# Products of two blocks of F in the second half of the opening, and the last six of the 32 steps of x's first transform stage left to the h/dh pass

## The chip, the cores and the metric

One core of a Trainium2 chip runs the kernel. The metric is device time in microseconds (us). Engines: PE is TensorE, DVE is VectorE, ACT is ScalarE, POOL is GpSimd. DMAs are issued from SP's and POOL's queues. "Granted clock" is the share of TensorE's full clock; it is taken from the trace.

## The reference, cut to what matters

```python
x = A_x
g = sigmoid((x * gate_w).sum(-1, keepdims=True))
a = irfft2(rfft2(x) * (w_r + 1j * w_i))          # spectral branch, S x D = 2048 x 1024
h = relu(x @ w1 + b1) ** 2                        # dense branch, F = 3584
b = h @ w2 + b2
out = g * a + (1 - g) * b
# returned: out, and the gradients of x, w_r, w_i, w1, b1, w2, b2, gate_w for a given grad_out
```

Both branches work on x (A_x); the input B_x takes no part. The kernel needs h and its gradient dh for all of F. It works them out in 14 blocks of 256 columns of F, each in 4 steps s of 512 rows, with 2 halves c.

## The kernel before: the parts that matter

Four stretches follow each other. In the **opening** (to about 85 us) x and grad_out come in, are scaled, transposed on PE into xT and dbT, and x's first transform stage (`first_stage_of_x`, 16 tiles) runs beside block 0 of the dense branch. A row step of that stage is some additions on DVE (the folds) and 8 products on PE; a column step is 8 products on PE, copies on ACT, two additions on DVE (the **u additions**) and a store of u to DRAM (the **z store**, `z_scr`). Two buffers hold u, so a u addition can have to wait for an earlier z store. In the **h/dh pass** the other blocks run beside the first stage of the gradient. Then come the pw products (weight gradients) beside the spectral middle, and at last the outputs.

```python
def hidden(fc, ss, w1g, h2T):              # "ph": 8 products of 512 columns, then ACT
    ph = mps.tile([P, SW], FP32, name="ph", tag="ph", bufs=2)
    ...
    nc.scalar.activation(rT[:], ph[:], ACT.Relu, bias=...)
    nc.scalar.activation(h2T, rT[:], ACT.Square)

def grads(fc, sb, ss, rT, dhT):            # "pd": 8 products, then DVE; shares ph's two PSUM buffers
    pd = mps.tile([P, SW], FP32, name="pd", tag="ph", bufs=2)
    ...
    return STT(out=dhT, in0=pd[:], scalar=2.0, in1=rT[:], ...)

# opening, once for each 4 tiles i0
gate(i0); next(stage); next(units); next(stage)
for k in (i0 // 2, i0 // 2 + 1):
    turned(dbT, k, ...); next(stage)       # transposes of dbn on PE, copies dbT<-pt on DVE
... x_pair(k), next(stage) twice           # transposes of x, copies on ACT
next(units); next(stage); next(stage)
# after it
for _ in stage: pass
first = first_stage_of_grad()
mixed = spread(units, first, 0.55)         # 0.55 side steps for each unit of the dense branch
while n < 78: ...
```

At fixed steps of a block, DVE also transposes h2T, dhT and w1 for later stages, and the w2 of the next group (a group is two blocks of F): `load_w2` loads it (`w2r`), `turn_group` turns it on DVE, `move` writes it over the w2T of this group.

Of the kernel before, what the change touches and what calls it, by code (L numbers as in the profile page):

```python
# [10 lines left out]
P = 128  # L11
BF16 = mybir.dt.bfloat16
# [113 lines left out]
def kernel(  # L126
# [22 lines left out]
    nc = tc.nc  # L149
# [7 lines left out]
    S2, DC, FC = g.S2, g.DC, g.FC  # L157
# [3 lines left out]
    FGW, FG, FGC = g.FGW, g.FG, g.FGC  # L161
# [55 lines left out]
    def after(ins, earlier, wait=mybir.DependencyClass.Sync):  # L217

        if earlier is not None:
            info = mybir.DependencyInfo(wait, mybir.DependencyReason.DATA)  # L220
            tc.add_manual_dep(ins.ins, earlier.ins.name, info, reason="paced")
# [420 lines left out]
    def mlp_in():  # L642
# [8 lines left out]
        def hidden(fc, ss, w1g, h2T):  # L651
            ph = mps.tile([P, SW], FP32, name="ph", tag="ph", bufs=2)
            for dc in range(DC):
                mm(ph[:], lhsT=w1g[:, dc, fc % 2 * P : (fc % 2 + 1) * P], rhs=xT[:, dc, ss], start=(dc == 0), stop=(dc == DC - 1))  # L654
            rT = wb.tile([P, SW], BF16, name="rT", tag="rT", bufs=3)
            nc.scalar.activation(rT[:], ph[:], ACT.Relu, bias=b1col[:, fc : fc + 1])  # L656
            nc.scalar.activation(h2T, rT[:], ACT.Square)  # L657
            return rT

        def grads(fc, sb, ss, rT, dhT):  # L660
            w_ = w2T[fc % FGC].bitcast(BF16)
            pd = mps.tile([P, SW], FP32, name="pd", tag="ph", bufs=2)
            for ec in range(DC):
                mm(  # L664
                    pd[:], lhsT=w_[:, ec // 2, ec % 2 :: 2], rhs=dbT[:, ec, ss],
                    start=(ec == 0), stop=(ec == DC - 1),
                )
            return STT(  # L668
                out=dhT, in0=pd[:], scalar=2.0, in1=rT[:], op0=ALU.mult, op1=ALU.mult,
                accum_out=gb1part[:, fc, sb : sb + 1],  # L670
            )
# [6 lines left out]
        def turn_w2(fc):  # L678
            w2r = wb.tile([P, D], BF16, name="w2n", tag="w2n", bufs=2)
            ld(out=w2r[:], in_=B_w2[fc * P : (fc + 1) * P, :])  # L680

            def turn():
                ptw = tps.tile([P, DC, P], BF16, name="ptw", tag="tr", bufs=2)
                for b in range(DC):
                    nc.tensor.transpose(ptw[:, b, :], w2r[:, of_tile(b)], identb[:])
                nc.vector.tensor_copy(
                    out=w2_tile(fc).bitcast(BF16).rearrange("p u (m c) -> p u c m", c=2),
                    in_=ptw[:].rearrange("p (u c) m -> p u c m", c=2),
                )

            return turn
# [19 lines left out]
                for b in range(4):  # L711
                    ld(out=t_[32 * b : 32 * (b + 1)], in_=v_[32 * a : 32 * (a + 1), :, b, :])

        for fp in range(FC // 2):
            w1g = wb.tile([P, DC, PW], BF16, name="w1g", tag="w1g", bufs=2)
            ld(out=w1g[:], in_=w1v[:, :, fp * PW : (fp + 1) * PW])
            fg, pr = divmod(fp, NPR)
            turns = []
            if fp == 0:
                turns = [turn_w2(0), turn_w2(1)]  # L720
            if fp == 0:
                yield
            step = 0
            for sp in range(2):
                cols2 = slice(2 * sp * SW, 2 * (sp + 1) * SW)
                h2T, dhT = (wb.tile([P, 2, 2 * SW], BF16, name=n_, tag=n_, bufs=2) for n_ in ("h2T", "dhT"))
                for sh in range(2):
                    sb = 2 * sp + sh
                    ss = slice(sb * SW, (sb + 1) * SW)
                    hs = slice(sh * SW, (sh + 1) * SW)  # L730
                    if fp == 0:
                        rT = [hidden(c, ss, w1g, h2T[:, c, hs]) for c in range(2)]
                        yield
                    for t_ in turns:
                        t_()
                    turns = []
                    if fp == 0 and sb == 1:
                        turns = [turn_w2(2), turn_w2(3)]
                    for c in range(2):
                        if fp > 0:  # L740
                            rT = {c: hidden(2 * fp + c, ss, w1g, h2T[:, c, hs])}
                        last = grads(2 * fp + c, sb, ss, rT[c], dhT[:, c, hs])
                        later["last"] = last
                        if 8 * pr + step == 3:
                            later["blocks"] = last
                        if step == 4:
                            st1 = wb.tile([P, 2, 4, DC, 32], BF16, name="stg1", tag="stg1", bufs=1)
                            turned_ = nc.vector.transpose(
                                out=st1[:].rearrange("p v b c i -> p c (v b) i"),
                                in_=w1g[:].rearrange("p c (b i) -> p c b i", i=32),  # L750
                            )
                            after(turned_, last, mybir.DependencyClass.NoSync)
                            st(
                                out=w1T_scr[2 * fp : 2 * fp + 2].rearrange("v p b r -> p v (b r)"),
                                in_=st1[:].rearrange("p v b c i -> p v (b c i)"),
                            )
                        if pr == 0 and step == 1 and fg > 0:
                            move((2, 3))
                        if fg + 1 < FG:
                            at = 8 * pr + step  # L760
                            if at == (7 if fg == 0 else 5):
                                for q in range(4):
                                    load_w2(fg + 1, q, last)
                            if at == 11:
                                for q in range(4):
                                    turn_group(q, last)
                                move((0, 1))
                        step += 1
                        if fp > 0 or c == 1:
                            yield  # L770
                stg = wb.tile([P, 16, 2, 32], I32, name="stg", tag="stg", bufs=3)
                for c in range(2):
                    nc.vector.transpose(  # L773
                        out=stg[:, :, c, :], in_=h2T[:, c, :].bitcast(I32).rearrange("p (b i) -> p b i", i=32)
                    )
                st(out=h2_scr[fg][:, 16 * sp : 16 * (sp + 1), 2 * pr : 2 * pr + 2, :], in_=stg[:])
                st(out=h2T_scr[2 * fp : 2 * fp + 2, :, cols2].rearrange("c p s -> p c s"), in_=h2T[:])
                stg = wb.tile([P, 4, 8, 2, 32], BF16, name="stgd", tag="stg", bufs=3)
                for c in range(2):
                    nc.vector.transpose(  # L780
                        out=stg[:, :, :, c, :].rearrange("p b k i -> p k b i"),
                        in_=dhT[:, c, :].rearrange("p (k b i) -> p k b i", b=4, i=32),
                    )
                st(
                    out=dh_scr[fg][:, :, pr, 8 * sp : 8 * (sp + 1), :].rearrange("p b k r -> p b (k r)"),
                    in_=stg[:].rearrange("p b k c i -> p b (k c i)"),
                )
                st(out=dhT_scr[2 * fp : 2 * fp + 2, :, cols2].rearrange("c p s -> p c s"), in_=dhT[:])
        mpss.close()
        wbs.close()  # L790
        xT_s.close()
# [226 lines left out]
    for i0 in range(0, NT, 4):  # L1018
        for i in range(i0, i0 + 4):
            ld(out=dbn[:, i, :], in_=go_perm[i])  # L1020
        if i0 + 4 < NT:
            for i in range(i0 + 4, i0 + 8):
                xs[i] = source(i, x_perm)
        gate(i0)
        next(stage, None)
        next(units)
        next(stage, None)
        for k in (i0 // 2, i0 // 2 + 1):
            turned(dbT, k, lambda i: dbn[:, i, :], of_tile, nc.vector.tensor_copy)
            next(stage, None)  # L1030
        if i0 + 4 < NT:
            for k in (i0 // 2 + 2, i0 // 2 + 3):
                x_pair(k)
                next(stage, None)
        next(units)
        next(stage, None)
        next(stage, None)
    for _ in stage:
        pass
    V(out=gpg[:], in0=gcol[:], in1=omg[:], op=ALU.mult)  # L1040
    first = first_stage_of_grad()
    n = 0
    mixed = spread(units, first, 0.55)
    while n < 78:
        next(mixed)
        n += 1
    for _ in first:
# [53 lines left out]
```

## Time and profile before

| what | before |
|---|---|
| time, median of the first 3 runs | 1335.81 us (1335.26 to 1336.68) |
| span of the profiled run | 1334.6 us |
| PE busy | 1298.0 us (97%) |
| DVE busy in the opening, 29 to 81 us | 50.86 of 52 us |
| first pw product starts at | 466.45 us |

The page's busy shares name the bound of the whole; the busy time of each engine in a stretch names the bound of that stretch, and here it is another one. The prediction shows these lines. One tool is used: the **loss**, which is the start of an instruction in the trace less all PE work that stands before it in the built order, at the streaming durations that the prediction lists. A loss that grows between two points is PE time that stood, or ran slowly, between them. It needs starts alone; PE busy times are less sure, as some PE records can be missing from a trace (the page of before has 6974 products for 7082 weight loads).

### The profile page before, as it was taken

The numbers are of one execution on the slowest core, as the hardware profiler recorded it, in microseconds if no ns is written. First come the engines' busy times: TensorE is split into PE (matmuls) and PEld (weight loads), VectorE is DVE, ScalarE is ACT, GpSimd is POOL, SyncE is SP. The second block draws the span as 40 slices with busy tenths as digits, with TensorE's granted clock in tenths as the row PEclk, the third lists the DMA queues.
The fourth block names the chain that finished last, engine by engine and source line by source line (L and its number), as shares of the span: only waits on it lengthen the run. The fifth ranks groups of instructions, "written<-read, shape, count | busy, mean of one in ns | idle before, by whom it ended". The sixth has DMA issues, their size and how long they took to land.

```text
span 1334.6 us, 18965 instructions
## 1 busy us (share of the span) xinstructions
PE 1298.0 (97%) x6974; PEld 630.2 (47%) x7082; DVE 836.0 (63%) x1669; ACT 424.5 (32%) x722; POOL 295.7 (22%) x484
## 2 busy tenths in 40 slices
PE   7889999999999999999999999999999899999998
PEld 4644444444444444444444445555444444444443
DVE  6986777676666596785667863434756776842232
ACT  6863555555433323232332323443111111000000
POOL 0222232232222253533442212121000000000000
PEclk9999999999999999999999999999999999999999
DMA  7547787788768988889886557778888854663530
GB/s 274 188 161 242 242 254 255 236 259 247 242 207 241 278 252 186 215 201 218 215 174 180 145 156 231 234 251 250 207 223 218 246 163 136 206 180 97 147 103 24
DMA packets 217094, 273.06 MB, mean 205 GB/s; under 512 B 16988, under 2 KB 152170, under 8 KB 217002
## 3 DMA queue, kind: packets, MB, share of 16 engines
q1 hardware_dynamic: 181306, 153.58, 43.4%
q0 software_dynamic: 35696, 118.27, 27.3%
q8 instruction: 55, 0.90, 0.3%
q14 instruction: 37, 0.30, 0.1%
HBM read 146.99 MB, written 118.51 MB: 199 GB/s over the span
## 4 chain that ended last, share of the span: by engine, by line
PE 83%; DVE 9%; DMA 3%; issue 2%; ACT 1%; POOL 1%; SPq 0%; DVEq 0%; ACTq 0%; POOLq 0%
PE accg L983 14%; PE acc L941 14%; PE pw L875 14%; PE ph L654 13%; PE pd L664 13%; PE pw L858 7%; DMA out_dram<-wo 2%; DVE dbacc L835 1%; PE pui L283 1%; DVE dbT L579 1%; PE pki L504 1%; PE pk L250 1%; DVE x L332 1%; PE pu L283 1%; DVE t L451 1%
## 5 line engine op out<-in xcount | busy, mean ns | idle before, releaser
L654 PE MATMUL ph<-xT,w1g 128*128 128x512 bf16 x869 | 215.6, 382 | 2.1 <-DMA w1g<-in_B_w_dram 0.7
L664 PE MATMUL pd<-dbT,w2T 128*128 128x512 bf16 x876 | 211.5, 381 | 3.9 <-DVE dhT L668 1.8
L875 PE MATMUL pw<-grd,res 128*128 128x512 bf16 x896 | 202.4, 379 | 0.0
L858 PE MATMUL pw<-dbn,grp 128*128 128x512 bf16 x875 | 199.9, 379 | 1.2 <-issue 0.2
L941 PE MATMUL acc<-w,hblk 128*128 128x512 bf16 x874 | 196.4, 379 | 3.0 <-DVE bGo L943 1.8
L983 PE MATMUL accg<-w1Tr,hblk 128*128 128x512 bf16 x878 | 192.9, 379 | 0.9
L664 PEld LDWEIGHTS <-w2T 128*128 128x128 bf16 x896 | 87.6, 98 | 107.8 <-issue 5.6
L983 PEld LDWEIGHTS <-hblk 128*128 128x128 bf16 x896 | 87.5, 98 | 105.8 <-issue 0.9
L858 PEld LDWEIGHTS <-grp 128*128 128x128 bf16 x896 | 86.8, 98 | 103.1 <-issue 0.9
L941 PEld LDWEIGHTS <-hblk 128*128 128x128 bf16 x896 | 86.6, 98 | 100.5 <-issue 1.9
L875 PEld LDWEIGHTS <-res 128*128 128x128 bf16 x896 | 86.0, 98 | 98.7 <-issue 0.7
L654 PEld LDWEIGHTS <-w1g 128*128 128x128 bf16 x896 | 86.1, 98 | 97.9 <-issue 2.1
L656 ACT ACTIVATE rT<-ph,b1col 128x512 bf16<-128x512 f32 x112 | 77.0, 687 | 142.6 <-PE ph L654 135.6
L668 DVE SCALAR_TENSOR_TENSOR dhT<-pd,rT 128x512 bf16<-128x512 f32 x112 | 75.1, 671 | 55.4 <-PE pd L664 46.0
L988 DVE TENSOR_TENSOR gxo<-accg,g 128x512 bf16<-128x512 f32 x32 | 22.1, 691 | 106.3 <-PE accg L983 100.7
L773 DVE STREAM_TRANSPOSE stg<-h2T 128x512 int32<-128x512 int32 x56 | 39.8, 711 | 64.4 <-ACT h2T L657 64.4
L862 ACT CAST wo<-pw 128x512 bf16<-128x512 f32 x56 | 32.7, 585 | 143.4 <-PE pw L858 127.5
L870 POOL DMA_DIRECT2D out_dram<-wo x112 | 56.0, 506 | 93.2 <-ACT wo L862 76.1
L880 ACT CAST wo<-pw 128x512 bf16<-128x512 f32 x56 | 32.8, 585 | 132.0 <-PE pw L875 103.0
L657 ACT ACTIVATE h2T<-rT 128x512 bf16<-128x512 bf16 x112 | 70.5, 630 | 3.1
L780 DVE STREAM_TRANSPOSE stgd<-dhT 128x1024 bf16<-128x1024 bf16 x56 | 69.3, 1240 | 1.2
L332 DVE TENSOR_TENSOR x<-px,common 128x1024 f16<-128x1024 f32 x32 | 38.8, 1220 | 45.3 <-ACT common L329 45.3
(182 smaller groups left out, 1488.8 us busy)
## 6 DMA issues: line engine op xcount, KB each, us to landing
h2T_scr<-h2T POOLq DMA_DIRECT2D x28, 512.0 KB, 4.6
h_scr<-stg POOLq DMA_DIRECT2D x28, 512.0 KB, 6.9
dhT_scr<-dhT POOLq DMA_DIRECT2D x28, 512.0 KB, 7.4
dh_scr<-stgd POOLq DMA_DIRECT2D x28, 512.0 KB, 7.1
grp<-h_scr SPq DMA_DIRECT2D x112, 128.0 KB
grd<-dh_scr SPq DMA_DIRECT2D x112, 128.0 KB
hblk<-h2T_scr SPq DMA_DIRECT2D x8, 1792.0 KB
hblk<-dhT_scr SPq DMA_DIRECT2D x8, 1792.0 KB
```

What stands on the lines that cost most here:

```text
L332: V(out=x[:, j, :, 0:H].rearrange("p c (i g) -> p c i g", g=4), in0=px[:].rearrange("p c (g i) -> p c i g", g=4), in1=common[:].rearrange( ...
L654: mm(ph[:], lhsT=w1g[:, dc, fc % 2 * P : (fc % 2 + 1) * P], rhs=xT[:, dc, ss], start=(dc == 0), stop=(dc == DC - 1))
L656: nc.scalar.activation(rT[:], ph[:], ACT.Relu, bias=b1col[:, fc : fc + 1])
L657: nc.scalar.activation(h2T, rT[:], ACT.Square)
L664: mm(pd[:], lhsT=w_[:, ec // 2, ec % 2 :: 2], rhs=dbT[:, ec, ss], start=(ec == 0), stop=(ec == DC - 1),)
L668: return STT(out=dhT, in0=pd[:], scalar=2.0, in1=rT[:], op0=ALU.mult, op1=ALU.mult, accum_out=gb1part[:, fc, sb : sb + 1],)
L780: nc.vector.transpose(out=stg[:, :, :, c, :].rearrange("p b k i -> p k b i"), in_=dhT[:, c, :].rearrange("p (k b i) -> p k b i", b=4, i=32),)
L858: mm(pw[:], lhsT=cur[:, t // 2, 2 * fb_ * P + t % 2 : 2 * (fb_ + 1) * P : 2], rhs=dbn[:, t, hf * H : (hf + 1) * H], start=(t == 0), stop=( ...
L870: st(out=dst[q], in_=wo[32 * q : 32 * (q + 1), :])
L875: mm(pw[:], lhsT=xr[t][:, d_ * P : (d_ + 1) * P], rhs=cur[:, t], start=(t == 0), stop=(t == NT - 1),)
L941: mm(acc[:], lhsT=cur[:, fc, t2::2], rhs=w2[:, fc, cs], start=(fc == 0), stop=(fc == FC - 1))
L983: mm(acc[:], lhsT=cur[:, fc, t2::2], rhs=w1T[:, fc, 2 * hf : 2 * hf + 2, :], start=(fc == 0), stop=(fc == FC - 1),)
```

## The change

PE waits for DVE in the opening and is full in the pass. So work that PE can do without much DVE is pulled forward from the pass, and work that costs DVE is pushed back. Core of the diff (cut; the bodies of `forth` and `back_` are the old loop's, taken apart):

```diff
+        for s in range(4):
+            both(forth, 0, s)                      # ph of block 0
+            yield
             ...
+            if s == 1:
+                load_w1(1)
+                turns = [turn_w2(2), turn_w2(3)]
+            if s >= 2:
+                both(forth, 1, s - 2)              # ph of block 1, first half
+            both(back_, 0, s)                      # pd of block 0
+            if s >= 2:
+                both(back_, 1, s - 2)              # pd of block 1, first half
+            yield
+        for fp in range(1, FC // 2):
+            ...
+            for s in range(2 if fp == 1 else 0, 4):
...
-                            if at == (7 if fg == 0 else 5):
+                if at == (4 if fg == 0 else 5):    # loads of the next group's w2
...
         next(units)
         next(stage, None)
-        next(stage, None)
-    for _ in stage:
-        pass
     V(out=gpg[:], in0=gcol[:], in1=omg[:], op=ALU.mult)
-    first = first_stage_of_grad()
+    def firsts():
+        yield from stage                           # what is left of x's stage: 4 column, 2 row steps
+        yield from first_stage_of_grad()
+    first = firsts()
-    mixed = spread(units, first, 0.55)
-    while n < 78:
+    mixed = spread(units, first, 0.62)
+    while n < 75:
```

More of the change, by code (lines that the diff above doesn't have):

```diff
@@ L712, in move @@
                     ld(out=t_[32 * b : 32 * (b + 1)], in_=v_[32 * a : 32 * (a + 1), :, b, :])
-        for fp in range(FC // 2):
-            w1g = wb.tile([P, DC, PW], BF16, name="w1g", tag="w1g", bufs=2)
-            ld(out=w1g[:], in_=w1v[:, :, fp * PW : (fp + 1) * PW])
-            fg, pr = divmod(fp, NPR)
-            turns = []
-            if fp == 0:
-                turns = [turn_w2(0), turn_w2(1)]
-            if fp == 0:
-                yield
-            step = 0
-            for sp in range(2):
-                cols2 = slice(2 * sp * SW, 2 * (sp + 1) * SW)
-                h2T, dhT = (wb.tile([P, 2, 2 * SW], BF16, name=n_, tag=n_, bufs=2) for n_ in ("h2T", "dhT"))
-                for sh in range(2):
-                    sb = 2 * sp + sh
-                    ss = slice(sb * SW, (sb + 1) * SW)
-                    hs = slice(sh * SW, (sh + 1) * SW)
-                    if fp == 0:
-                        rT = [hidden(c, ss, w1g, h2T[:, c, hs]) for c in range(2)]
-                        yield
-                    for t_ in turns:
-                        t_()
-                    turns = []
-                    if fp == 0 and sb == 1:
-                        turns = [turn_w2(2), turn_w2(3)]
-                    for c in range(2):
-                        if fp > 0:
-                            rT = {c: hidden(2 * fp + c, ss, w1g, h2T[:, c, hs])}
-                        last = grads(2 * fp + c, sb, ss, rT[c], dhT[:, c, hs])
-                        later["last"] = last
-                        if 8 * pr + step == 3:
-                            later["blocks"] = last
-                        if step == 4:
-                            st1 = wb.tile([P, 2, 4, DC, 32], BF16, name="stg1", tag="stg1", bufs=1)
-                            turned_ = nc.vector.transpose(
-                                out=st1[:].rearrange("p v b c i -> p c (v b) i"),
-                                in_=w1g[:].rearrange("p c (b i) -> p c b i", i=32),
-                            )
-                            after(turned_, last, mybir.DependencyClass.NoSync)
-                            st(
-                                out=w1T_scr[2 * fp : 2 * fp + 2].rearrange("v p b r -> p v (b r)"),
-                                in_=st1[:].rearrange("p v b c i -> p v (b c i)"),
-                            )
-                        if pr == 0 and step == 1 and fg > 0:
-                            move((2, 3))
-                        if fg + 1 < FG:
-                            at = 8 * pr + step
-                            if at == (7 if fg == 0 else 5):
-                                for q in range(4):
-                                    load_w2(fg + 1, q, last)
-                            if at == 11:
-                                for q in range(4):
-                                    turn_group(q, last)
-                                move((0, 1))
-                        step += 1
-                        if fp > 0 or c == 1:
-                            yield
-                stg = wb.tile([P, 16, 2, 32], I32, name="stg", tag="stg", bufs=3)
-                for c in range(2):
-                    nc.vector.transpose(
-                        out=stg[:, :, c, :], in_=h2T[:, c, :].bitcast(I32).rearrange("p (b i) -> p b i", i=32)
-                    )
-                st(out=h2_scr[fg][:, 16 * sp : 16 * (sp + 1), 2 * pr : 2 * pr + 2, :], in_=stg[:])
-                st(out=h2T_scr[2 * fp : 2 * fp + 2, :, cols2].rearrange("c p s -> p c s"), in_=h2T[:])
-                stg = wb.tile([P, 4, 8, 2, 32], BF16, name="stgd", tag="stg", bufs=3)
-                for c in range(2):
-                    nc.vector.transpose(
-                        out=stg[:, :, :, c, :].rearrange("p b k i -> p k b i"),
-                        in_=dhT[:, c, :].rearrange("p (k b i) -> p k b i", b=4, i=32),
-                    )
-                st(
-                    out=dh_scr[fg][:, :, pr, 8 * sp : 8 * (sp + 1), :].rearrange("p b k r -> p b (k r)"),
-                    in_=stg[:].rearrange("p b k c i -> p b (k c i)"),
-                )
-                st(out=dhT_scr[2 * fp : 2 * fp + 2, :, cols2].rearrange("c p s -> p c s"), in_=dhT[:])
@@ new lines, in mlp_in, with load_w1, forth @@
+        w1, h2, dh, rTs = {}, {}, {}, {}
+        wide = lambda n_: wb.tile([P, 2, 2 * SW], BF16, name=n_, tag=n_, bufs=2)
+        rows_ = lambda s: slice(s * SW, (s + 1) * SW)
+        def load_w1(fp):
+            w1[fp] = wb.tile([P, DC, PW], BF16, name="w1g", tag="w1g", bufs=2)
+            ld(out=w1[fp][:], in_=w1v[:, :, fp * PW : (fp + 1) * PW])
+        def forth(fp, s, c):
+            if c == 0 and s % 2 == 0:
+                h2[fp, s // 2], dh[fp, s // 2] = wide("h2T"), wide("dhT")
+            rTs[fp, s, c] = hidden(2 * fp + c, rows_(s), w1[fp], h2[fp, s // 2][:, c, rows_(s % 2)])
@@ new lines, in back_ @@
+        def back_(fp, s, c):
+            fg, pr = divmod(fp, NPR)
+            step = 2 * s + c
+            last = grads(2 * fp + c, s, rows_(s), rTs.pop((fp, s, c)), dh[fp, s // 2][:, c, rows_(s % 2)])
+            later["last"] = last
+            if 8 * pr + step == 3:
+                later["blocks"] = last
+            if step == 4:
+                st1 = wb.tile([P, 2, 4, DC, 32], BF16, name="stg1", tag="stg1", bufs=1)
+                turned_ = nc.vector.transpose(
+                    out=st1[:].rearrange("p v b c i -> p c (v b) i"),
+                    in_=w1[fp][:].rearrange("p c (b i) -> p c b i", i=32),
+                )
+                after(turned_, last, mybir.DependencyClass.NoSync)
+                st(
+                    out=w1T_scr[2 * fp : 2 * fp + 2].rearrange("v p b r -> p v (b r)"),
+                    in_=st1[:].rearrange("p v b c i -> p v (b c i)"),
+                )
+            if pr == 0 and step == 1 and fg > 0:
+                move((2, 3))
+            if fg + 1 < FG:
+                at = 8 * pr + step
+                if at == (4 if fg == 0 else 5):
+                    for q in range(4):
+                        load_w2(fg + 1, q, last)
+                if at == 11:
+                    for q in range(4):
+                        turn_group(q, last)
+                    move((0, 1))
+            if c == 1 and s % 2 == 1:
+                finish(fp, s // 2)
@@ new lines, in finish @@
+        def finish(fp, sp):
+            fg, pr = divmod(fp, NPR)
+            cols2 = slice(2 * sp * SW, 2 * (sp + 1) * SW)
+            h2T, dhT = h2.pop((fp, sp)), dh.pop((fp, sp))
+            stg = wb.tile([P, 16, 2, 32], I32, name="stg", tag="stg", bufs=3)
+            for c in range(2):
+                nc.vector.transpose(
+                    out=stg[:, :, c, :], in_=h2T[:, c, :].bitcast(I32).rearrange("p (b i) -> p b i", i=32)
+                )
+            st(out=h2_scr[fg][:, 16 * sp : 16 * (sp + 1), 2 * pr : 2 * pr + 2, :], in_=stg[:])
+            st(out=h2T_scr[2 * fp : 2 * fp + 2, :, cols2].rearrange("c p s -> p c s"), in_=h2T[:])
+            stg = wb.tile([P, 4, 8, 2, 32], BF16, name="stgd", tag="stg", bufs=3)
+            for c in range(2):
+                nc.vector.transpose(
+                    out=stg[:, :, :, c, :].rearrange("p b k i -> p k b i"),
+                    in_=dhT[:, c, :].rearrange("p (k b i) -> p k b i", b=4, i=32),
+                )
+            st(
+                out=dh_scr[fg][:, :, pr, 8 * sp : 8 * (sp + 1), :].rearrange("p b k r -> p b (k r)"),
+                in_=stg[:].rearrange("p b k c i -> p b (k c i)"),
+            )
+            st(out=dhT_scr[2 * fp : 2 * fp + 2, :, cols2].rearrange("c p s -> p c s"), in_=dhT[:])
@@ new lines, in mlp_in @@
+        both = lambda what, fp, s: [what(fp, s, c) for c in range(2)]
+        load_w1(0)
+        turns = [turn_w2(0), turn_w2(1)]
+        yield
+        for s in range(4):
+            both(forth, 0, s)
+            yield
+            for t_ in turns:
+                t_()
+            turns = []
+            if s == 1:
[6 more added lines that the diff above has]
+                both(back_, 1, s - 2)
+            yield
@@ L789, in mlp_in @@
+        for fp in range(1, FC // 2):
+            if fp > 1:
+                load_w1(fp)
+            for s in range(2 if fp == 1 else 0, 4):
+                for c in range(2):
+                    forth(fp, s, c)
+                    back_(fp, s, c)
+                    yield
         mpss.close()
```

## The prediction

> **What bounds the kernel now.** I read the page's busy shares first, then the stretches of time around the opening, then PE's and DVE's waits there, then PE's instructions in order of time.
>
> ```profile
> PE 1298.0 (97%) x6974; PEld 630.2 (47%) x7082; DVE 836.0 (63%) x1669; ACT 424.5 (32%) x722; POOL 295.7 (22%) x484
> ```
>
> PE (TensorE) is the bound over the whole, so only time in which PE stands or runs slowly can be won: 1334.6 - 1298.0 = 36.6 us in all. The stretches say where that lies (columns: stretch, length, busy of PE, PEld, DVE, ACT, POOL, granted clock, DMA share, GB/s):
>
> ```profile
> 29.00:81.00 52.00, 45.36 (x534) 31.90 (x540) 50.86 (x121) 39.49 (x86) 10.30 (x16) 1.00 0.57 191
> 81.00:99.50 18.50, 16.59 (x101) 8.44 (x101) 12.73 (x35) 10.96 (x23) 4.38 (x7) 0.91 0.47 151
> 99.50:130.00 30.50, 30.28 (x138) 13.78 (x141) 18.50 (x31) 11.15 (x17) 7.81 (x10) 1.00 0.82 250
> ```
>
> From 29 to 81 us, the opening, DVE is busy 50.86 of 52 us and PE stands 6.6 us: DVE is the bound there. From 99.5 us on, in the h/dh pass, PE is busy 30.28 of 30.5 and DVE only 18.5: PE is the bound and DVE has room. The waits before 100 us (us in total, times, longest) name it:
>
> ```profile
> PE pt L578 <- DVE dbT L579: 7.6, 9, 1.8
> PE pd L664 <- DVE dhT L668: 1.5, 1, 1.5
> ...
> DVE u L270 <- DMA z_scr<-u: 4.4, 1, 4.4
> ```
>
> PE's transposes of dbn/x wait for DVE to empty the two PSUM buffers (dbT copies, 1.13 us each from start to start). At the end of the opening PE's rows are
>
> ```profile
> 77.18 0.61 PE L578 MATMUL pt<-identb,dbn 128*128 128x128 bf16 x8 [0.88 <-DVE dbT L579]
> 79.58 0.61 PE L578 MATMUL pt<-identb,dbn 128*128 128x128 bf16 x8 [1.80 <-DVE dbT L579]
> ...
> 82.12 4.38 PE L664 MATMUL pd<-dbT,w2T 128*128 128x512 bf16 x14 [0.22 <-issue]
> ...
> 99.53 1.89 PE L664 MATMUL pd<-dbT,w2T 128*128 128x512 bf16 x8 [1.54 <-DVE dhT L668]
> ...
> 466.45 13.98 PE L858 MATMUL pw<-dbn,grp 128*128 128x512 bf16 x62
> ```
>
> and the granted clock falls just behind those waits:
>
> ```profile
> 81.00:83.00 2.00, 1.78 (x11) 0.90 (x10) 2.00 (x6) 1.88 (x3) 0.00 (x0) 0.53 0.01 4
> 83.00:85.00 2.00, 2.00 (x7) 0.78 (x6) 1.28 (x4) 0.41 (x2) 0.54 (x1) 0.62 0.23 86
> ```
>
> The row at 466.45 is my marker. In the built programs PE does exactly the same work before the first pw product in both kernels (896 ph, 896 pd, 256 + 256 products of the first transform stage, 289 transposes, 32 of w2, 128 of the gate), only in another order, and PE's order behind the marker is the same instruction for instruction. So the change moves the marker, and the rest should follow it.
>
> **What PE loses before the marker.** From starts in the trace: a 512-wide product takes 0.2158 us in a stream (eight from 104.71 to 106.44), a transpose 0.064, a gate product 0.028, one of the first stage 0.056 (rows) or 0.066 (columns). The PE work ahead of the marker then sums to 440.0 us, against 466.45: 26.4 lost. Walking the sum along the trace: 14.9 lost by the first pd at 28.94 (first loads, ramp, short waits), 21.7 by the last dbT transposes at 79.58, 25.6 by the pd at 99.53, 26.4 at the marker. So **6.8 us** go in the middle of the opening, **3.9** just behind it (about 1.7 by the halved clock from 81 to 85, 1.5 by the wait at 99.53, the rest small), 0.8 in the whole pass after it.
>
> **What the Trainium skill says.** "TensorE: Matmul & The Clock Gate", section "Wait — 56ns, not 53.3ns?", gives 215.7 ns between 512-wide products at full clock; the trace has 216. Its section "What's actually happening" says an idle window of about 3.4 us halves the clock: the trace shows 0.53 and 0.62 for some 4 us, though PE's longest idle gap was 1.80 us, so here low activity was enough. "Perfetto Trace Analysis", section "Optimization Strategy", advises interleaving regimes whose most contended engines differ; that is this change. The section "Architectural detail: the array is 16× 32×32, not 1× 128×128" says DVE's queue is strictly first in, first out: the trace agrees, for the u addition that waited 4.44 us for a z store held up the dhT product behind it, and PE 1.54 us behind that.
>
> **The change part by part.**
> 1. In the second half of the opening the steps s = 2 and 3 of block 0 are joined by s = 0 and 1 of block 1: 4 ph and 4 pd groups of 8 products, 8 x 8 x 0.2158 = 13.8 us of PE work, taken from the pass where PE is full. By the last dbT transposes the built order has 20 ph and 16 pd products more than before: 36 x 0.2158 = 7.8 us. The rest (28) comes right behind, where PE used to start cold and wait.
> 2. Four column steps and two row steps of x's first stage go to the pass: 6 steps of about 0.5 us PE, and 4 x 0.4 us plus up to 2 x 1.76 us of DVE. PE does them either way; in the pass DVE is 60 to 87% busy, so they fit.
> 3. DVE before the last dbT copy, counted in the built orders: 2 more dhT products (0.61 each), 2 more of each first fold (4 x 0.337), one more transpose of h2T (0.63), one pair of u additions less (0.40): +2.8 us. The scheduler moves the x fold operations early, so the opening is not lighter on DVE, but slightly heavier.
> 4. The ratio 0.62 for 0.55 side steps a unit serves 46 steps in 75 units where 40 were served; the weight loads come one step earlier or later. No PE cost.
>
> **The sum.** If DVE stays the bound, the last dbT transposes come 2.8 us later, at 82.4, with 7.8 us more PE work done: loss there 21.7 + 2.8 - 7.8 = 16.7, so 5.0 won. Behind them PE has 12 ph products (2.6 us) to cover the last copies, is less idle ahead, so the half clock (1.7) should mostly go, and the burst of u stores that made the 1.5 us wait is spread out. Against it: DVE now leaves the opening with a backlog (8 dhT products, 4 pairs of transposes, the four w2 transposes and a w1 transpose, some 16 us within 20 us of PE time), and with two PSUM buffers for ph and pd a late dhT product stops PE; I count about 1.2 us of such stops, and guess 1.5 for PE and DVE waiting on each other in the denser opening. 5.0 + 3.2 - 1.2 - 1.5 = **5.5 to 6 us** won. 1335.8 - 5.8 = **1330.0 us**.
>
> **Rivals.** (a) *DVE backlog becomes the new wait*: h2T/dhT transposes of two blocks crowd the same 20 us, PE waits on dhT where it waited on dbT, and only 1 or 2 us are won: 1334. For it: DVE at 98% in the opening, and part 3. Against: at the same stage PE had almost nothing to fill the gaps with. (b) *Everything is filled*: loss after 28.94 falls to nearly nothing, 10 us won: 1325.5. For it: 7.8 us of work go into 6.8 us of gaps. Against: DVE's own floor. (c) *Stores collide*: eight more 0.5 MB stores in or near the opening delay z stores, and a 4 us DVE wait as at 98 us comes twice, or w2r loads for the next group come late: time unchanged or 1 to 2 us longer, 1336 to 1338. For it: that wait exists. Against: DMA share is only 0.57 in the opening. (d) *The gain is hidden later*: unlikely, since PE is 98% busy behind the marker (852.0 of 868.15 us) and its waits there are local.
>
> **Range and chances.** The ledger caps the gain at 10.6 us plus little, so 1325 is the floor; a loss needs a new wait of over 6 us. Eight in ten: 1325.5 to 1335.0. A step of 2% is 26.7 us, all that PE loses before the marker, so neither verdict of change is likely: faster 0.01, same 0.98, slower 0.01.
>
> **What would show it.** Right: PE's waits for dbT before 100 us fall from 7.6 to under 4; the clock stays at 1.0 between 75 and 95 us; first pw product at about 460.5; behind it the same 868 us. DVE still near full up to about 85. Part 3 is wrong if the last dbT copy ends much before or after 85; part 1 if PE waits on pd for dhT by more than 3 us after it. The prediction is wrong if the stretch behind the marker changes by over 2 us, or the pass at 100 to 460 shows PE waits of over 2 us.

## The result, and the profile after

The changed kernel took 1331.2 us (median of 4 runs, 1328.97 to 1331.76) against 1335.53 us (1333.9 to 1336.68, 4 runs). The ratio is 0.9965 with a 95% interval of 0.9948 to 0.9983: within 2%, and faster by some 4.7 us. (Ratios are the mean time of one kernel's fast runs over that of the other's fast runs of the same rounds, so not quite the ratio of the medians.) The stretches of the changed kernel, in the columns of the prediction:

```profile
29.00:81.00 52.00, 47.27 (x498) 30.48 (x496) 49.25 (x122) 36.88 (x81) 8.85 (x13) 1.00 0.48 166
81.00:99.50 18.50, 18.28 (x135) 10.25 (x134) 17.26 (x32) 9.77 (x19) 7.01 (x9) 1.00 0.73 234
99.50:130.00 30.50, 30.45 (x171) 15.09 (x169) 18.60 (x37) 15.98 (x25) 9.40 (x13) 1.00 0.84 235
```

From 29 to 81 us PE is busier (47.27 for 45.36) and DVE less (49.25 for 50.86). The larger step is the second row: 18.28 for 16.59 us of PE, and the clock is 1.00 where it was 0.91. PE's waits before 100 us (us in total, times, longest):

```profile
PE pt L578 <- DVE dbT L579: 3.5, 6, 0.9
PE pt L578 <- ACT xT L579: 2.7, 4, 0.9
```

The waits for dbT have halved, from 7.6 us, and the wait for dhT is gone. PE's rows at the end of the opening, and the marker:

```profile
77.68 3.62 PE L654 MATMUL ph<-xT,w1g 128*128 128x512 bf16 x16
81.14 0.68 PE L283 MATMUL pu<-cf,ft 128*128 128x256 f16 x8
81.66 1.05 PE L578 MATMUL pt<-identb,dbn 128*128 128x128 bf16 x16
82.55 0.61 PE L250 MATMUL pk<-kf,f 128*128 128x128 f16 x8
...
85.16 0.61 PE L578 MATMUL pt<-identb,dbn 128*128 128x128 bf16 x8
85.61 2.75 PE L654 MATMUL ph<-xT,w1g 128*128 128x512 bf16 x12
88.20 1.89 PE L664 MATMUL pd<-dbT,w2T 128*128 128x512 bf16 x8
...
460.20 13.98 PE L879 MATMUL pw<-dbn,grp 128*128 128x512 bf16 x64
```

None of these rows has a wait behind it in brackets, and of the five left out ahead of 85.16 only one has (0.18 us): each starts when the one before lets it. The marker, the first pw product, moved from 466.45 to 460.20 us. Behind it stand 869.0 us (1329.2 - 460.2) against 868.15.

The losses at four points ("behind first pd" is marker less first pd, and is free of how soon the first loads arrive):

| kernel | first pd | last gate | last dbT transposes | marker | behind first pd | marker at |
|---|---|---|---|---|---|---|
| before | 15.0 | 18.7 | 21.7 | 26.4 | **11.4** | 466.45 |
| before, again (e14) | 13.8 | 17.6 | 20.6 | 25.0 | **11.2** | 465.02 |
| after | 14.0 | 19.5 | 19.5 | 20.2 | **6.2** | 460.20 |
| after, again (e3) | 15.1 | 21.0 | 21.0 | 21.7 | **6.6** | 461.74 |
| e1 products alone | 13.9 | 20.7 | 20.7 | 23.5 | 9.6 | 463.54 |
| e2 stage move alone, 0.62 | 12.0 | 18.3 | 19.4 | 29.4 | 17.4 | 469.38 |
| e12 stage move alone, 0.55 | 13.5 | 18.1 | 19.3 | 24.5 | 11.0 | 464.49 |
| e7 before + PE dose | 13.6 | 16.7 | 19.0 | 22.3 | 8.7 | 464.99 |
| e8 after + PE dose | 13.8 | 19.4 | 19.4 | 20.3 | 6.5 | 462.96 |
| e9 before + DVE dose | 14.3 | 19.6 | 25.5 | 30.0 | 15.7 | 470.00 |
| e10 after + DVE dose | 13.8 | 19.2 | 19.5 | 20.3 | 6.5 | 460.29 |
| e13 after, w2 loads at step 7 | 14.7 | 20.2 | 20.2 | 37.7 | 23.0 | 477.71 |
| e11 block 1 one step earlier | 14.3 | 21.6 | 21.7 | 37.8 | 23.5 | 477.82 |

Between the last gate and the last dbT transposes the loss grows by 3.0 us before and 0.0 after. From there to the marker it grows by 4.7 and 4.4 before, 0.7 and 0.7 after. From the first pd to the last gate it grows by more after (5.5, 5.9) than before (3.7, 3.8).

### The profile page after: what moved, and what is told of

The parts are those of the page before. It is cut to its first block, busy times and chain, and to the rows that moved or that the text cites. A ratio compares the mean times of both kernels' runs of the same rounds, so it can differ in the third digit from the quotient of the medians.

```text
span 1329.2 us, 19067 instructions
## 1 busy us (share of the span) xinstructions
PE 1303.1 (98%) x7082; PEld 630.2 (47%) x7082; DVE 835.6 (63%) x1669; ACT 423.7 (32%) x722; POOL 295.2 (22%) x484
## 4 chain that ended last, share of the span: by engine, by line
PE 87%; DVE 6%; DMA 3%; ACT 2%; issue 1%; SPq 0%; POOL 0%; DVEq 0%; ACTq 0%; POOLq 0%
PE acc L962 15%; PE accg L1004 15%; PE pd L664 14%; PE ph L654 14%; PE pw L896 14%; PE pw L879 8%; PE pui L283 1%; DMA z<-z_scr 1%; PE pki L504 1%; PE pk L250 1%; PE pu L283 1%; DMA out_dram<-wo 1%; DVE t L451 1%; DVE dbT L579 1%; DVE t L450 1%
## 5 line engine op out<-in xcount | busy, mean ns | idle before, releaser
L654 PE MATMUL ph<-xT,w1g 128*128 128x512 bf16 x896 | 219.1, 381 | 0.5 <-DMA w1g<-in_B_w_dram 0.5
L962 PE MATMUL acc<-w,hblk 128*128 128x512 bf16 x896 | 199.9, 381 | 1.8 <-DVE bGo L964 1.8
L1004 PEld LDWEIGHTS <-hblk 128*128 128x128 bf16 x896 | 87.5, 98 | 105.8 <-issue 0.9
```

The lines of the kernel that those rows point to most:

```text
L654: mm(ph[:], lhsT=w1g[:, dc, fc % 2 * P : (fc % 2 + 1) * P], rhs=xT[:, dc, ss], start=(dc == 0), stop=(dc == DC - 1))
L962: mm(acc[:], lhsT=cur[:, fc, t2::2], rhs=w2[:, fc, cs], start=(fc == 0), stop=(fc == FC - 1))
L1004: mm(acc[:], lhsT=cur[:, fc, t2::2], rhs=w1T[:, fc, 2 * hf : 2 * hf + 2, :], start=(fc == 0), stop=(fc == FC - 1),)
```

## The experiments

Theory A: the gain is PE work put where PE stood or ran slowly. Theory B: it is the u additions and their z stores taken out of the end of the opening.

**e1, products alone.** Block 1 joins as in the change; x's stage stays in the opening at the old ratio.

```diff
+        next(stage, None)
+    for _ in stage:
+        pass
-    mixed = spread(units, first, 0.62)
+    mixed = spread(units, first, 0.55)
```

> The products of block 1 join the opening's second half, but x's first stage stays wholly in the opening. Theory A (the gain is PE work put into a stretch where PE stood idle or ran at half clock): most of the gain is here already, first pw product at 460 to 462 us against 466.45 before and 460.2 after, time 4 to 6 us under the kernel before. Theory B (the gain comes from taking u additions and their stores out of the end of the opening, so that DVE no longer waits for a z store): no gain or at most 2 us, first pw at 464.5 to 466.5, and the long DVE wait for a z store is still there.

1334.69 us, ratio 0.9982 (0.9969 to 0.9995), first pw at 463.54. The loss between the last gate and the last transposes is 0.0, as after, but 2.8 us go behind them. The first line is ACT's wait there, the second PE's row behind it:

```profile
ACT u L264 <- DMA z_scr<-u: 3.8, 1, 3.8
...
111.80 1.89 PE L654 MATMUL ph<-xT,w1g 128*128 128x512 bf16 x8 [1.22 <-ACT rT L656]
```

ACT stands 3.8 us for a z store, the relu behind it is late, and PE waits 1.2 us for that; the rest of the 2.8 is in smaller steps. Neither theory alone: the products win 1.7 us behind the first pd (11.3 to 9.6), and the burst of u steps keeps a wait alive.

**e2 and e12, the stage move alone.** The old block loop, with the tail of the change; e2 at ratio 0.62, e12 at 0.55.

```diff
-        next(stage, None)
-    for _ in stage:
-        pass
-    first = first_stage_of_grad()
+    first = firsts()
-    mixed = spread(units, first, 0.55)
+    mixed = spread(units, first, 0.62)      # e12: 0.55, and 86 units in place of 78
```

> Only x's last column steps move to the h/dh pass; the products of block 1 stay in the pass. Theory A: 1 to 2.5 us faster than before (the 1.5 us PE wait behind the z store goes), first pw at 464 to 465.5, and PE still waits about 7 us for the dbT copies. Theory B: 4 to 6 us faster, first pw at 460.5 to 462.5.

1338.79 us, ratio 1.0018 (1.0003 to 1.0032), first pw at 469.38: slower, which neither theory foresaw. The profiled run is the slowest of its five (1342.35), and 1.7 us of its loss is a half-clock stretch at 58 us, ahead of all that the ratio touches. PE's waits in the pass of e2:

```profile
164.25 1.89 PE L664 MATMUL pd<-dbT,w2T 128*128 128x512 bf16 x8 [0.78 <-ACT rT L656]
...
225.16 1.89 PE L664 MATMUL pd<-dbT,w2T 128*128 128x512 bf16 x8 [0.87 <-DVE dhT L668]
286.27 1.89 PE L664 MATMUL pd<-dbT,w2T 128*128 128x512 bf16 x8 [0.87 <-DVE dhT L668]
347.39 1.89 PE L664 MATMUL pd<-dbT,w2T 128*128 128x512 bf16 x8 [0.87 <-DVE dhT L668]
```

A wait comes back every 61 us, once for each group of two blocks, so it is tied to something that a group does once (DVE's four transposes of w2, from 219.57 on, run ahead of the wait at 225.16). The changed kernel has the same ratio 0.62 and no such wait. e12 asked whether the ratio is at fault.

> Only the stage move, as e2_stage, but with the side steps at the old ratio 0.55 (86 units). e2_stage waited 0.87 us for dhT once in every 61 us of the pass, 5.5 us in all. If the denser side stream made those waits, they are gone here: PE waits in the pass under 1 us, first pw at 463.5 to 466, time 0 to 2 us under before. If they come from the moved steps themselves, they stay: 468 or later.

1335.74 us, ratio 0.9999 (0.9977 to 1.0020), first pw at 464.49, no PE wait in the pass behind 120 us. So the denser side stream cost e2 its time in the pass: from the last dbT transposes to the marker the loss grows by 10.0 us in e2 and 5.2 in e12. The moved steps alone, as built here, are worth nothing measurable (11.0 against 11.3 us behind the first pd). But one wait is left, ahead of 120 us. PE's row and DVE's wait, of 60 to 120 us:

```profile
107.03 1.89 PE L664 MATMUL pd<-dbT,w2T 128*128 128x512 bf16 x8 [1.66 <-DVE dhT L668]
```

```profile
DVE stg L702 <- DMA w2r<-in_B_w_dram: 1.5, 1, 1.5
```

The wait for the z store is gone, as Theory A said, and one for the w2 loads has taken its place. e2 and e12 have the old load step 7; with the u steps out of the way DVE reaches the transposes of w2 at 100.8 us (105.8 before), and the last of the four loads, issued from 85.5 us on, lets it go on at 104.1. Without that wait the move alone would have won about 1.8 us (an estimate: 0.3 and the 1.5 of DVE's wait), not the 4 to 6 of Theory B, so Theory B alone falls all the same. In the kernel before DVE has no wait for w2r at all, so the early loads by themselves have nothing to win there. Why 0.62 fits the changed kernel's order of units and not the old one was not tried.

**e3, the changed kernel again.**

> The changed kernel once more, unchanged, in the same rounds as the others: both theories 4 to 6 us under before, first pw at 460 to 462 us. The spread between two profiles of one kernel shows how far a single look can be trusted.

1332.32 us (1330.02 to 1338.35, 6 runs), ratio 0.9967 (0.995 to 0.9985), first pw at 461.74. The profiled run was the 1338.35 one, and its trace says why:

```profile
610.00:620.00 10.00, 8.75 (x31) 3.51 (x32) 3.99 (x7) 1.76 (x3) 1.96 (x4) 0.66 1.01 246
...
1040.00:1050.00 10.00, 8.77 (x28) 3.38 (x28) 8.25 (x28) 0.58 (x2) 1.62 (x3) 0.66 0.73 179
```

Two stretches far behind the change ran at half clock for 6.8 us each (a mean of 0.66 over 10 us is 6.8 us at 0.5), up to 3.4 us lost in each. The first look at the same kernel had only one, of 3.4 us, between 1034 and 1040 us. That is the spread of one kernel, and the reason for judging by the marker and the loss beside the time.

**e7 to e10, doses: which engine bounds the second half of the opening?** The row products of tiles 8 to 13 are done twice (2.7 us of PE), or their first fold addition three times (4.1 us of DVE); the results stay the same.

```diff
+            for _ in range(extra):          # PE dose, extra = 1 for tiles 8 to 13
+                mm(pk[:, b, :], lhsT=f[:, row, o], rhs=kmat, start=True, stop=True)
...
+        for _ in range(extra):              # DVE dose, extra = 2 for tiles 8 to 13
+            V(out=f[:, 0:2, 1:Q], in0=a0, in1=a1, op=ALU.add)
```

> The kernel before, with the 8 row products of tiles 8 to 13 of x's first stage done twice (6 x 8 x 0.056 = 2.7 us more PE work in the opening's second half, same result). If DVE bounds that stretch in the kernel before, PE has room and the dose is hidden: first pw at 465.5 to 467.5 (464 if the extra activity keeps the clock up), time within 1 us of before. If PE were the bound there, first pw at 469.

> The changed kernel with the same PE dose of 2.7 us. If the change has filled PE (new theory: PE, not DVE, bounds the second half of the opening now), the dose is paid in full: first pw 2.2 to 2.9 us later than in the two looks at after (460.2 and 461.7), at 462.5 to 464.5. If DVE still bounds it (the prediction's step), it is mostly hidden: at most 1 us later.

> The kernel before with the first fold addition of tiles 8 to 13 done three times (12 x 0.34 = 4.1 us more DVE work in the opening's second half, same result). If DVE is the bound there before: first pw 3 to 4 us later, at 469.5 to 470.5, and more PE waits for dbT. If not: under 1.5 us later.

> The changed kernel with the same DVE dose of 4.1 us. If PE is the bound in the second half now, DVE has some slack and part is hidden: first pw 0 to 2 us later than after. If DVE is still the bound: 3 to 4 us later.

| dose | on | ratio to before | loss behind first pd | without dose |
|---|---|---|---|---|
| 2.7 us PE | before (e7) | 0.9997 (0.9981 to 1.0014) | 8.7 | 11.3 |
| 2.7 us PE | after (e8) | 0.9974 (0.9958 to 0.9991) | 6.5 | 6.4 |
| 4.1 us DVE | before (e9) | 1.0027 (1.0008 to 1.0046) | 15.7 | 11.3 |
| 4.1 us DVE | after (e10) | 0.9970 (0.9949 to 0.9992) | 6.5 | 6.4 |

The PE dose is counted as work, so a loss that stays (e8) means that it was paid in full, and one that falls by 2.6 us (e7) that it was hidden. About 1.7 us of those 2.6 is the half-clock stretch, which e7's trace does not have; only the rest went into time in which PE stood. So e7 alone says little of DVE, and e9 is the stronger evidence. The DVE dose is not counted, so e9 paid 4.4 us and e10 nothing. Of the 4.4, 1.7 is a second half-clock stretch at 60 us, perhaps chance, as e2 has one at 58 us without a dose; from the last gate to the last dbT transposes alone the loss grows by 5.9 us for 3.0 before. The stretch rows of e9 and e10, in that order:

```profile
29.00:81.00 52.00, 44.59 (x510) 31.48 (x513) 50.55 (x124) 39.12 (x82) 9.84 (x15) 0.97 0.55 183
```

```profile
29.00:81.00 52.00, 46.56 (x487) 30.26 (x492) 50.38 (x128) 36.80 (x79) 8.89 (x13) 1.00 0.48 162
```

In this fixed window DVE is busy alike in both, and yet its dose costs nothing in e10, because the window does not hold the same work. From the first pd to the end of the last dbT copy (`--windows` with these two times) DVE is busy 52.1 of 53.3 us before and 56.0 of 59.3 after: it had 3.4 us to spare after, and 1.1 before. The dose makes that stretch 4.4 us longer in e9 (57.7 us) and 0.1 us in e10 (59.5 us). So the bound of that half was DVE before, and **PE after**.

**e13, the w2 loads back at step 7.** The one-character part of the diff that I had called free.

```diff
-                if at == (4 if fg == 0 else 5):
+                if at == (7 if fg == 0 else 5):
```

> The changed kernel with the first group's w2 loads back at step 7. They are then issued in the same step as the transposes that read them. If that load time matters, DVE stands behind the w2r loads as in e6_earlier (12 us there) and PE behind DVE: first pw 3 to 12 us later than after. If it was a detail: 460 to 462.

1348.71 us, ratio 1.0089 (1.0058 to 1.012), first pw at 477.71, 16 to 17.5 us later than in the two looks at after and so more than expected. PE's wait and DVE's, of the stretch behind the opening:

```profile
PE pd L664 <- DVE dhT L668: 15.0, 1, 15.0
```

```profile
DVE stg L702 <- DMA w2r<-in_B_w_dram: 14.5, 4, 6.8
```

Pulling half of block 1 forward also pulls forward the DVE transposes of the next group's w2 (about 98 us after, 105.8 us before). In the changed kernel its loads are issued from 72.2 us on and DVE finds them there. With the old step they are issued at 94.2 us; DVE, in order, stands 14.5 us in front of them with the dhT product behind, and PE with it. The step number is not a detail: without it the change would lose some 12 us in place of winning 4.7.

**e6 and e11, one step more.** Block 1 joins from s = 1 on (cut; the same for its pd, its w1 load one step earlier, ratio 0.63 and 74 units).

```diff
-            if s >= 2:
-                both(forth, 1, s - 2)
+            if s >= 1:
+                both(forth, 1, s - 1)
```

> Block 1 joins one step earlier (steps s = 1 to 3 of block 0 with s = 0 to 2 of block 1; ratio 0.63, 74 units), so 13.8/2 = 6.9 us more PE work moves into the opening. If PE still has room there (what the prediction said: DVE is the bound), first pw comes another 2 to 3 us earlier, at 457 to 458.5. If PE is already full in the second half and only the first half has idle time left (4.9 us lost between 28 and 63.5 us in the trace of after), it gains at most 1.5 us; if the added DVE work (two more dhT products, more h2T and dhT transposes) holds up the dbT copies, it gains nothing: 460 to 462.

The result was wrong (relative error 0.19), by a mistake of mine: the next group's w2 was moved over w2T before block 0's last pd had read it. Its times (1349.81 us) say nothing of the idea; DVE stood 12.0 us for w2r loads there as well. e11 puts the turn and the move two products later for the first group (13 in place of 11) and is correct.

> The earlier join again (block 1 from step s = 1 of block 0), with the error of e6_earlier mended: for the first group the transposes of the next group's w2 and their moves wait until two products later (at 13 in place of 11), so no block 0 product reads overwritten weights and DVE does not stand behind w2r loads. The doses showed PE full in the second half of after; only the first half still loses about 5 us (14.0 at the first pd, 19.5 at the last gate). If the added work fills that: first pw at 457.5 to 459.5. If it only moves the queue: 460 to 462. If the denser DVE work delays the dbT copies or the later w2 move makes pd wait: later than 462.

1345.35 us, ratio 1.0076 (1.0054 to 1.0098), first pw at 477.82. The opening loses 7.4 us from the first pd to the last dbT transposes (after: 5.5 and 5.9; 1.7 of it in a half-clock stretch at 48.8 us), so the first half was not filled, and behind it two waits are new:

```profile
100.97 3.57 PE L664 MATMUL pd<-dbT,w2T 128*128 128x512 bf16 x8 [3.54 <-DVE stg L765]
...
129.18 1.44 PE L664 MATMUL pd<-dbT,w2T 128*128 128x512 bf16 x3 [4.42 <-DMA w2T<-stg]
```

In the trace the first stands behind a DVE wait of 3.4 us for a z store. The second is the price of the later move. With the two come two half-clock stretches of 6.8 us. Whether an earlier join with w2 handled otherwise would win is left open. No experiment beat the changed kernel. (There is no e4 or e5. A variant with a fourth rT buffer, as I noted, did not fit into SBUF and was not run; the record does not hold it.)

**e14, before again.**

> A second look at the kernel before. If its half clock behind the last dbT waits is a habit and not chance, there is a stretch of about 3.4 us at half clock between 50 and 90 us again and the first pw is at 465.5 to 467.5. If it was chance, the clock stays at 1.00 there and the first pw is at 464 to 465.5.

1336.51 us (one run), first pw at 465.02, and the half clock is there again:

```profile
76.00:78.00 2.00, 0.61 (x8) 0.48 (x8) 1.89 (x6) 0.87 (x4) 0.57 (x1) 1.00 0.81 305
78.00:80.00 2.00, 1.54 (x15) 1.54 (x15) 2.00 (x5) 0.20 (x1) 0.00 (x0) 0.57 0.37 139
80.00:82.00 2.00, 1.89 (x14) 1.42 (x13) 1.47 (x3) 1.64 (x3) 0.00 (x0) 0.57 0.02 4
```

A clock of 0.57 over 4 us is 3.4 us at half speed, 1.7 us of full-speed work. Kernels with the old block loop show such a stretch between 50 and 90 us in five of six looks (before, e2, e9, e12, e14; not e7, the PE dose); those with block 1 joined as in the change in none of six (after, e1, e3, e8, e10, e13); e11, which joins earlier, has one at 48.8 to 52.2 us. So it goes with the thin end of the old opening.

## Why the prediction was right, and where its steps were not

The time (1330.0 against 1331.2), the marker (460.5 against 460.20 and 461.74), the side of the waits for dbT (3.5 us, under 4) and the clock were right, and rivals (a) and (c), no gain through a DVE backlog or colliding stores, fell for the kernel as built. Rival (b), everything filled, came true for the second half of the opening only. The ledger holds too: the win behind the first pd is 11.3 - 6.4 = 4.9 us, all of it ahead of the marker. (Two readings of the prediction's text: its 289 transposes include the 32 of w2, as its sum of 440.0 us has them; and the section on DVE's queue that it names stands in "TensorE: Matmul & The Clock Gate".)

Two terms of the sum were mis-sized, in opposite directions, and hid each other. That the total came so close is luck in part.

- *"If DVE stays the bound, the last dbT transposes come 2.8 us later, at 82.4 ... so 5.0 won."* DVE did not stay the bound. The transposes came at 85.16, and from the first pd to them the loss fell only from 6.7 and 6.8 to 5.5 and 5.9 us: about 1 us won. The second half won its 3.0 us whole, as PE was full there, which e8 and e10 show by dose. The first half lost 2 us more than before. In the traces PE's waits for dbT there fell from 3.1 to 1.6 us, but those for ACT (xT, u, f) rose from 0.3 to 2.8; why ACT came later was not tested. The sign set for part 3 was missed by 2 to 4 us as well: the last dbT copy ended at 87.32 and 88.87 us, not 85. From the first pd to that end DVE's busy time grew by 3.9 us (2.8 were counted), the time by 6.1. I had counted DVE's work up to the last copy and not asked whether PE's own queue, with 7.8 us more in it, would become longer than DVE's.
- *"5.0 + 3.2 - 1.2 - 1.5"*: behind the transposes this leaves 0.5 us won. Measured: 4.55 to 0.7, so 3.85 us. The 1.7 us of half clock and the 1.5 us behind the z store went, as said. But the stops by late dhT products and by mutual waiting did not come: PE has one wait of 0.2 us in all between 75 and 455 us, for u, and none for dhT, and the DVE dose of 4.1 us brought one of 0.2 us only.
- *Parts 1 and 2 as separate gains.* Alone they win 1.7 us (e1) and 0.3 us (e12), together 4.9. The 0.3 holds the wait for late w2 loads; without it about 1.8 (the estimate above), so 1.4 of the 4.9 us would be left to the two together, and not 2.9. The products need the u steps gone, or a z store stops ACT and PE; the moved steps only pay once PE has something to do in their place.
- *Part 4, "the weight loads come one step earlier or later. No PE cost."* True of the kernel as built, and missed in substance: it is the part without which the rest loses (e13). Rival (c) had named late w2r loads; I did not see that the load step was what kept them away.

## What to carry to other kernels

Count the work of both engines up to the same point before saying which one ends a stretch: filling an idle engine can make it the bound there, and a small dose of idempotent work on each engine tells which it is in two runs. Compare an engine's reserve over the same work, not over the same window of time. When work is pulled forward, list everything that is tied to its step number: a load that was early enough becomes late, and on an engine that works in order that stops all that stands behind it. Test a part of a change alone only with what it depends on: e12 left the early loads out, and their wait hid what the move had won. A gain of a third of a per cent is read at a marker behind the change and from a ledger of losses more sharply than from the end-to-end time.

## What the Trainium skill lacked or had wrong

- "TensorE: Matmul & The Clock Gate", section "HAM oscillation — how this bites in real kernels", gives "no PE-idle gaps >~3.4µs" as the rule. Here the clock halved for 3.4 us with no gap above 1.80 us between 10 and 81 us; in the 3.4 us ahead of it PE was busy 1.57 us (before) and 0.89 us (e14). The page's next section does tell of a kernel in which short idle times between groups of products made the clock swing, but gives no share of busy time. Much of PE's work there is transposes; whether they count like other products was not tested.
- The same page, section "Back-to-back issue gap", gives about 131 ns for 512-wide and 81 ns for 128-wide products in a real stream. The traces show 216 ns (8 in 1.73 us) and 56 ns (8 row products in 0.45 us), which the section gives for the isolated case.
- No page says how much half-clock stretches in the middle of a kernel spread its time (the first page speaks of the ramp at the start): the changed kernel ran from 1330.02 to 1338.35 us in one set of rounds, and its slowest run had 13.7 us of half clock far behind the change.
- No page ties a load's lead to an in-order engine: issued at 94.2 in place of 72.2 us, four w2 loads held DVE for 14.5 us and PE for 15.0 us.
